# Earlier loads and an earlier dispatch in the last block of an attention and soft-MoE kernel

## The chip, the cores and the metric

One core of one Trainium2 chip runs the whole program. The metric is the device time of one execution in microseconds (us). A time given as "at 525.7" counts from the first instruction of the profiled execution.

## What is computed

Three layers follow each other, all in 32-bit floats.

```python
# q, k, v: (8, 8, 576, 64), attention inside chunks of 64 tokens
scores = q_c @ k_c.T / sqrt(64);  out = softmax(scores) @ v_c
x = out.transpose(0, 2, 1, 3).reshape(4608, 512)
# first MLP
h = x @ w_in                              # 512 -> 2048
x = (h / (1 + exp(-1.702 * h))) @ w_out   # 2048 -> 512
# soft mixture of experts, 8 experts of 4 slots
logits = x @ phi                          # (4608, 32)
d = softmax(logits, axis=0)               # dispatch weights, over all tokens
slot_in = d.T @ x                         # (32, 512)
slot_out[e] = relu(slot_in[e] @ w1[e]) @ w2[e]   # w1: 512x1024, w2: 1024x512
out = softmax(logits, axis=1) @ slot_out  # combine weights, over the slots
```

## The kernel before

The 4608 tokens are cut into 12 blocks of 384 (block 0 to block 11). A block has 16 columns, one for each 128 features of the first MLP. `block(b)` runs the columns in order: `gemm(b, f)` does the 12 matmuls of column f, the tanh on ScalarE and the gelu product on VectorE; then `side(b, f)` adds what a hand-written plan puts at that column, and `at` issues the weight loads that `TABLE` names for it. The order of calls is the order of instructions on every engine. Nothing is reordered later; an instruction starts when its data and its buffer are there and its engine's queue has come to it.

`w_out` is not applied to the tokens. The dispatch works on the gelu values: `dispatch(b)` multiplies the block's dispatch weights with the gelu values turned by 90 degrees and adds the result to `acc`, and `w_out` comes once at the end. The turned gelu goes a long way in blocks 1 to 10: `store_g` turns 32x32 squares on VectorE into a buffer for 4 columns (`g1`), and stores it to DRAM in four transfers of 192 KB; in the block after, `load_g` loads the four quarters (`g2`, 768 KB each) back. In the last block there is no block after, so `gemm_t` turns the gelu on TensorE, two columns late, and VectorE copies it out.

For block b the steps of the softmax over tokens and slots are run in block b+1: `S0` (`slots_0`: the logits by one matmul, their maximum, a transposed copy), `S1` (`slots_1`: two exponentials on ScalarE), `S2` (`slots_2`: the dispatch weights `dt`, turned by four VectorE instructions), `S3` and `S4` (`slots_3`, `slots_b`: the combine weights, normalized, turned and stored to `ct_dram` in small pieces of 128 bytes by three transfers). `d0` is the dispatch and `g0` the load of the gelu. `PLAN` holds the columns for the ordinary blocks, `LAST` those of block 11. So block 11 does the work of block 10's softmax and dispatch, its own logits (`l0` to `l2`) and its own gemm.

The experts' weights (33.5 MB) are loaded from block 9 on into whatever buffer comes free. `TABLE` gives the order of buffer kinds: `w` is a buffer of `w_in` that a column of block 11 has used up, `s` a slab, `m` a small buffer, and so on. The loads of blocks 10 and 11 are issued by GpSimd, one behind the other, each waiting for its buffer. Gelu stores, gelu loads and combine-weight stores are issued by SyncE in the order of the program.

There are 11 slabs (`NSLAB`). The two halves of a block's tokens (`xh`, `xl`), `g1`, `g2`, the turned gelu of the last block (`g2t`, one slab for 4 columns), the `s` loads and the output tiles share them.

The `tail()` turns block 11's last columns, does its softmax and dispatch, applies `w_out`, runs the experts (`up`, `turn`, `down`) and combines. The twelve output tiles of 768 KB are stored by GpSimd (the first nine) and SyncE (the last three).

Of the kernel before, what the change touches and what calls it, by code (L numbers as in the profile page):

```python
# [17 lines left out]
T = 384  # L18
# [5 lines left out]
NW = 17  # L24
ROOM = {'w': 4, 's': 6, 'q': 4, 'v': 2, 'x': 2, 'p': 6, 'm': 2, 't': 2, 'k': 2, 'c': 4}
TABLE = {
    '9.15': 'cwxx', '10.6': 'q', '10.11': 'vq', '10.12': 't', '10.14': 'sst', '10.15': 'v', '11.0': 'w', '11.3': 's', '11.10': 'ss',
    'a': 'ssmk', 'b': 'ssss', 'e': 'ppppp',
}
TABLE.update({f'11.{f}': TABLE.get(f'11.{f}', '') + 'w' for f in range(1, 16)})  # L30
TABLE.update({f'11.{f}': TABLE[f'11.{f}'] + 'm' for f in range(10, 16)})
TABLE['11.15'] += 'm'
TABLE['11.5'] = ''.join(TABLE.pop(f'11.{f}') for f in (2, 3, 4, 5))
EVAC = 'vvvvvvvvvvvvvvav'
LAST = (('g0', 2), ('l3', 4), ('l0', 4), ('S0', 5), ('S1', 6), ('S2', 7), ('S3', 8), ('S4', 8), ('d0', 9), ('l1', 8), ('l2', 12))

# [50 lines left out]
def attention_moe_softmoe_kernel(  # L89
# [16 lines left out]
    NF = DFF // 128  # L106
    NB = NT // T
    NCP = T // 128
    GF = 4
    NG = NF // GF  # L110
# [19 lines left out]
    def slab_tile(shape, dtype, name):  # L130
        return slab.tile(shape, dtype, tag="s", name=name)
# [186 lines left out]
    def attn_e(cp, pool):  # L318
        exp(cp)
        for _ in steps_f(cp, pool):  # L320
            pass
# [35 lines left out]
    def attn_b(cp):  # L357
        if cp >= TURN:
            t = pt[cp] = ptp.tile([128, 2 * KD, 64], F32, tag="p", name="pt_sb")
            nc.vector.transpose(out=t.rearrange("p a k -> p (a k)"), in_=et.pop(cp).rearrange("p a k -> p (a k)"))  # L360
        else:
            attn_t(cp)
            attn_p(cp)
# [69 lines left out]
    gt, g1, g2, g2t, gh = {}, {}, {}, {}, {}  # L433
# [45 lines left out]

    g_dram = {}  # L480

    def load_g(b):
        g2[b] = []
        for q in range(NG):
            t = slab_tile([128, 4, NCP, GF * 32], F32, f"g2_{q}")
            nc.sync.dma_start(
                out=t.rearrange("p q a c -> p (q a c)"), in_=g_dram.pop((b, q)).rearrange("b p q x -> (b p) (q x)")
            )
            g2[b].append([t[:, :, i, :] for i in range(NCP)])
# [20 lines left out]
    def logits(b, g):  # L510
        if g == 0:
            lp[b] = ps.tile([128, T], F32, tag="lp" if b % 2 or b == 0 else "pt", name="lp")
        for j in range(4):
            f = 4 * g + j
            nc.tensor.matmul(  # L515
                out=lp[b][32 * j:32 * (j + 1), :], lhsT=wp[:, f, :], rhs=gt[b, f],
                start=(g == 0), stop=(g == NG - 1),
            )
        if g == NG - 1:
            p = lp.pop(b)  # L520
            if b == NB - 1:
                lps[b] = [mid_tile([128, T], "lps")]
                nc.scalar.activation(out=lps[b][0], in_=p, func=ACTF.Copy)
                return
            lps[b] = [
                mid_tile([128, T], f"lps{i}", F32R) if b else pro[0].tile([128, T], F32R, tag="gt", name="lps0", bufs=NF)
                for i in range(2)
            ]
            nc.scalar.activation(out=lps[b][0], in_=p, func=ACTF.Copy)
            nc.vector.tensor_tensor(out=lps[b][1], in0=p, in1=lps[b][0].bitcast(F32), op=ALU.subtract)  # L530
# [101 lines left out]
    def slots_n(b):  # L632
        lt = lg_t[b]
        cs = st_p.tile([128, NCP, 1], F32, tag="cs", name="cs")
        nc.vector.tensor_reduce(out=cs, in_=lt, axis=AX.X, op=ALU.add)
        nc.vector.tensor_scalar_add(out=cs, in0=cs, scalar1=EPS)
        nc.vector.reciprocal(out=cs, in_=cs)
        nc.vector.tensor_tensor(out=lt, in0=lt, in1=cs.to_broadcast([128, NCP, 32]), op=ALU.mult)

    def slots_b(b):  # L640
        slots_n(b)
        lt = lg_t[b] if b == NB - 2 else lg_t.pop(b)
        t = st_p.tile([128, NCP, 32], F32, tag="ct", name="ct_b")
        nc.vector.transpose(out=t, in_=lt)
        for a in range(NCP):
            k, r = divmod(b * NCP + a, 4)
            if k == NT // 512 - 1:
                continue
            nc.sync.dma_start(out=ct_dram[r, :, k].rearrange("s j c -> j s c"), in_=t[:, a, :])

    def dispatch(b):
        dt, cr = dt_t.pop(b)
        g = g2.pop(b)
        p = ps.tile([128, 512], F32, tag="m", name="dtg")
        for i in range(NCP):
            for j in reversed(range(4)):
                nc.tensor.matmul(  # L657
                    out=p[32 * j:32 * (j + 1)], lhsT=dt[:, i, :], rhs=g[j][i], start=(i == 0), stop=(i == NCP - 1)
                )
        if b == FIRST:  # L660
            nc.vector.tensor_copy(acc, p)
        else:
            nc.vector.scalar_tensor_tensor(out=acc, in0=acc, scalar=cr, in1=p, op0=ALU.mult, op1=ALU.add)
# [94 lines left out]
    def more_wo():  # L758
        if wo_list:
            fn, i = wo_list.pop(0)  # L760
            fn(i)
# [227 lines left out]
    def side(b, f):  # L989
        for name, at in (LAST if b == NB - 1 else PLAN):  # L990
            if b == 2:
                at = {"g0": 9, "d0": 15, "b1": 5}.get(name, at)
            if b == 3:
                at = {"b3": 14}.get(name, at)
            if f != at:
                continue
            kind, i = name[0], int(name[1:])
            if kind == "l":
                if i == NG - 1:
                    logits(b - 1, i)  # L1000
                else:
                    logits(b, i)
            elif kind == "S":
                (slots_0, slots_1, slots_2, slots_3, slots_b)[i](b - 1)
            elif kind == "d":
                dispatch(b - 1)
            elif kind == "g":
                load_g(b - 1)
            elif kind == "w":
                if NPRO <= b < 10:  # L1010
                    more_wo()
            elif kind == "p":
                cp = (b + 1) * NCP + i
                pair_step(cp if cp < NB * NCP else None, cp - 2)
            elif (b + 1) * NCP + i < NB * NCP:
                cp = (b + 1) * NCP + i
                if kind == "e":
                    attn_e(cp, True)
                else:
                    attn_b(cp)  # L1020
# [15 lines left out]
    def pair_step(a, c, early=False):  # L1036
        t = pair_tile("sx")
        if a is not None:
            y = attn_s(a, t[:, :, 0:256])
        if c is not None:  # L1040
            z = attn_x(c, t[:, :, 256:512])
        if early and c is not None:
            attn_y(c, z)
        if a is not None:
            attn_m(a, y)
            if a > 5:
                load_qk(a + 2)
        if c is not None:
            if not early:
                attn_y(c, z)  # L1050
            if c > 5:
                load_v(c + 2)
# [67 lines left out]
    def start(steps):  # L1120
        fns = {
            "i": w_in_a, "h": w_in_h, "I": w_in_b, "j": w_in_c, "u": w_in_d, "o": wp_a, "q": load_qk, "v": load_v, "b": attn_b, "c": wp_c, "d": wp_d,
            "W": spin, "t": lambda f: store_g(0, f), "k": lambda g: logits(0, g), "l": lambda g: logits(1, g),
            "S": lambda i: (slots_0, slots_1, slots_2, slots_3, slots_b)[i](0),
        }
        once = {
            "phi": start_wp, "z": start_const, "s": start_sel, "G": lambda: load_g(0), "D": lambda: dispatch(0),
        }
        for x in steps.split():
            k, n = x[0], x[1:].rstrip("rp")  # L1130
            if x in once:
                once[x]()
            elif k == "L":
                load_w(x[1], int(n[1:]), x[-1])
            elif k == "P":
                pair_step(*[None if y == "-" else int(y) for y in n.split(",")], early=True)
            elif k == "e":
                attn_e(int(n), x[-1] != "r")
            else:
                fns[k](int(n))  # L1140
# [15 lines left out]
    def block(b):  # L1156
        for f in range(NF):
            gemm(b, f)
            if b == NB - 1 and f > 1:
                gemm_t(b, f - 2)  # L1160
            side(b, f)
            if b < 5:
                start((SIDE2, SIDE3, SIDE4)[b - 2].get(f, ""))
            at(f"{b}.{f}")
# [87 lines left out]
```

## Time and profile before

| | us |
|---|---|
| median of 3 runs | 626.5 (624.05 to 626.56) |
| the profiled execution's own time | 625.01 |
| its span, first to last instruction | 623.2 |
| TensorE busy | 606.0 |
| VectorE busy | 471.6 |
| ScalarE busy | 217.3 |
| GpSimd busy | 182.5 |

The span is what the trace covers; about 1.8 us of the execution's own time lie outside it. TensorE (PE) is busy in 97% of the span. Its granted clock is 0.995 of full speed over the span.

### The profile page before, as it was taken

The page shows a single profiled execution, that of the slowest core. Times are in us where ns is not written, and L with a number is a line of the kernel's source. Part 1 is how long each engine was busy: PE and PEld are TensorE (multiplying, and loading weights), DVE is VectorE, ACT ScalarE, POOL GpSimd, SP SyncE. Part 2 cuts the span into 40 slices and gives each one's busy share as a digit, 9 for nine tenths or more (in the row PEclk, how much of TensorE's full clock was granted, in tenths as well). Part 3 has the DMA queues.
Part 4 walks back from the last instruction along what each step waited for, and adds up shares of the span by engine and source line. Part 5 has one row for each costly group of instructions (what it writes and reads, how often), then busy time and mean ns, then how long its engine had stood idle before and what let it go on. Part 6 is the DMA issues. An engine that isn't in the chain of part 4 may idle for free.

```text
span 623.2 us, 15697 instructions
## 1 busy us (share of the span) xinstructions
PE 606.0 (97%) x6430; PEld 515.4 (83%) x6430; DVE 471.6 (76%) x1007; ACT 217.3 (35%) x461; POOL 182.5 (29%) x299
## 2 busy tenths in 40 slices
PE   8999999999999999999999999999999999989993
PEld 7899888888898798898979889989989798766652
DVE  6999698789788888998888889888877746343152
ACT  4986345232232332322333332423322322121152
POOL 1010010334134134154143333342441331353320
PEclk9999999999999999999999999999999999999998
DMA  8983785559799686795695794876839889899998
GB/s 343 398 313 122 232 306 152 134 134 363 189 358 290 230 279 217 199 339 179 183 348 169 238 325 146 289 241 166 329 96 305 288 259 414 293 356 411 409 390 336
DMA packets 64535, 167.81 MB, mean 269 GB/s; under 512 B 11536, under 2 KB 34064, under 8 KB 64464
## 3 DMA queue, kind: packets, MB, share of 16 engines
q1 hardware_dynamic: 54864, 127.75, 61.9%
q0 software_dynamic: 9600, 39.06, 16.3%
q8 instruction: 50, 0.82, 0.5%
q14 instruction: 21, 0.17, 0.1%
HBM read 122.22 MB, written 44.56 MB: 268 GB/s over the span
## 4 chain that ended last, share of the span: by engine, by line
PE 89%; DMA 7%; DVE 1%; SPq 1%; ACT 0%; issue 0%; DVEq 0%; ACTq 0%
PE h L445 62%; PE lp L515 5%; PE dtg L657 5%; DMA g<-g_dram 5%; PE sx L294 3%; PE fp L897 2%; PE h1p L859 2%; PE sx L387 2%; PE op L972 2%; DMA stg<-in_moe_w_in_dram 2%; DMA qv<-in_qk_dram 1%; PE wpp L238 1%; PE sx L400 1%; PE sip L812 1%; PE pt L372 1%; PE lg L538 1%
## 5 line engine op out<-in xcount | busy, mean ns | idle before, releaser
L445 PE MATMUL h<-xh,w 128*128 128x384 f32 x1536 | 396.2, 339 | 1.2 <-ACT xh L424 1.2
L445 PEld LDWEIGHTS h<-xh,w 128*128 128x128 f32 x1536 | 273.7, 188 | 26.6 <-issue 22.7
L445 PE MATMUL h<-xl,w 128*128 128x384 f32 x768 | 256.8, 335 | 0.0
L352 POOL TENSOR_TENSOR es<-e,rs 32x256 f32<-32x256 f32 x208 | 131.0, 630 | 242.9 <-DVE rs L335 193.1
L454 ACT ACTIVATE gt<-h 128x384 f32<-128x384 f32 x192 | 93.7, 489 | 221.9 <-PE h L445 221.7
L458 DVE SCALAR_TENSOR_TENSOR gt<-gt,h 128x384 f32<-128x384 f32 x192 | 103.4, 539 | 56.6 <-ACT gt L454 55.6
L445 PEld LDWEIGHTS h<-xl,w 128*128 128x128 f32 x768 | 144.1, 188 | 0.1
L467 DVE STREAM_TRANSPOSE g<-gt 128x384 f32<-128x384 f32 x176 | 100.5, 575 | 7.4 <-PE dtg L657 1.8
L424 ACT ACTIVATE xh<-sx 128x512 fp32r<-128x512 f32 (+1 forms) x38 | 21.5, 574 | 74.9 <-DVE e L313 44.3
L341 POOL TENSOR_TENSOR e<-e,rs 128x512 f32<-128x512 f32 x9 | 10.3, 1146 | 100.8 <-DVE rs L335 88.9
L515 PE MATMUL lp<-gt,wp 128*32 128x384 f32 x384 | 39.0, 493 | 0.0
L429 DVE TENSOR_TENSOR xl<-sx,xh 128x512 fp32r<-128x512 f32 (+1 forms) x38 | 24.8, 657 | 18.3 <-ACT xh L424 17.6
L657 PE MATMUL dtg<-g,dt 128*32 128x512 f32 x264 | 31.0, 596 | 1.7 <-DMA g<-g_dram 1.7
L737 POOL DMA_DIRECT2D w<-in_moe_w_dram x33 | 17.7, 538 | 45.7 <-PE h L445 26.9
L310 DVE TENSOR_REDUCE mx<-sx 128x8 f32<-128x512 f32 (+1 forms) x38 | 23.8, 631 | 7.0 <-PE sx L294 7.0
L313 DVE TENSOR_TENSOR e<-sx,mx 128x512 f32<-128x512 f32 (+1 forms) x38 | 25.0, 662 | 1.2
L325 ACT ACTIVATE e<-e 128x512 f32<-128x512 f32 x36 | 22.6, 628 | 7.6 <-DVE e L313 7.4
L743 POOL DMA_DIRECT2D w<-in_moe_w_dram x33 | 17.6, 535 | 22.0 <-DMA w<-in_moe_w_dram 13.3
L330 DVE TENSOR_REDUCE sm<-e 128x8 f32<-128x512 f32 x36 | 23.4, 650 | 0.0
L294 PEld LDWEIGHTS sx<-qk 64*64 64x64 f32 x960 | 16.7, 134 | 7.7 <-issue 7.4
L515 PEld LDWEIGHTS lp<-gt,wp 128*32 128x32 f32 x384 | 10.7, 109 | 13.1 <-issue 8.6
L657 PEld LDWEIGHTS dtg<-g,dt 128*32 128x32 f32 x264 | 8.2, 109 | 15.9 <-issue 13.8
(132 smaller groups left out, 546.1 us busy)
## 6 DMA issues: line engine op xcount, KB each, us to landing
g_dram<-g SPq DMA_DIRECT2D x176, 192.0 KB, 3.4
g<-g_dram SPq DMA_DIRECT2D x44, 768.0 KB, 8.7
w<-in_moe_w_dram POOLq DMA_DIRECT2D x37, 512.0 KB, 7.4
qk<-in_qk_dram SPq DMA_DIRECT2D x30, 512.0 KB, 10.3
stg<-in_moe_w_in_dram SPq DMA_DIRECT2D x16, 512.0 KB, 6.1
stg<-in_moe_w_out_t_dram SPq DMA_DIRECT2D x16, 512.0 KB, 5.6
wo<-in_moe_w_out_dram SPq DMA_DIRECT2D x16, 512.0 KB, 3.7
v<-in_v_dram SPq DMA_DIRECT2D x30, 256.0 KB, 8.5
```

The lines of the kernel that those rows point to most:

```text
L294: nc.tensor.matmul(out=y[h][w, hp, :], lhsT=t[r, 0, hp, w], rhs=t[r, 1, hp, w], start=True, stop=True)
L310: nc.vector.tensor_reduce(out=mx[:, hs], in_=v, axis=AX.X, op=ALU.max)
L313: nc.vector.tensor_tensor(out=ev[:, hs], in0=v, in1=mx[:, hs].to_broadcast(list(v.shape)), op=ALU.subtract)
L330: nc.vector.tensor_reduce(out=sm, in_=e, axis=AX.X, op=ALU.add)
L352: nc.gpsimd.tensor_tensor(out=t[w, :, 32 * i:32 * i + 32], in0=e[r, :, 32 * j:32 * j + 32], in1=rs[r].to_broadcast([32, 2 * KD, 32]), op=A ...
L429: nc.vector.tensor_tensor(out=l, in0=v, in1=h.bitcast(F32), op=ALU.subtract)
L445: nc.tensor.matmul(out=h, lhsT=w_t[f][:, (0, 1, 0)[p], k, :], rhs=(xh, xh, xl)[p][b][:, k, :], start=(i == 0), stop=(i + 1 == len(steps)),)
L454: nc.scalar.activation(out=gt[b, f], in_=gh[b, f], func=ACTF.Tanh, scale=0.851)
L458: nc.vector.scalar_tensor_tensor(out=t, in0=t, scalar=1.0, in1=gh.pop((b, f)), op0=ALU.add, op1=ALU.mult)
L467: nc.vector.transpose(out=g1[b, q][:, :, :, 32 * j:32 * (j + 1)], in_=t.rearrange("p (a b c) -> p b a c", b=4, c=32))
L515: nc.tensor.matmul(out=lp[b][32 * j:32 * (j + 1), :], lhsT=wp[:, f, :], rhs=gt[b, f], start=(g == 0), stop=(g == NG - 1),)
L657: nc.tensor.matmul(out=p[32 * j:32 * (j + 1)], lhsT=dt[:, i, :], rhs=g[j][i], start=(i == 0), stop=(i == NCP - 1))
```

## The change

Four things are changed in the last block and around it.

1. The load of block 10's gelu is split. Quarters 0, 1 and 2 (`G0`, `G1`, `G2`) are issued at column 0 of block 11, quarter 3 (`G3`) at column 2. Before, all four were issued at column 2.
2. `S4` of block 9, which normalizes and stores its combine weights, goes from column 15 of block 10 to column 0 of block 11, behind `G0` to `G2` (`T0`).
3. The dispatch of block 10 (`d0`) goes from column 9 to column 7, `S1` from 6 to 5, `S2` from 7 to 6.
4. In the table of weight loads one slab of the first two at the tail's start (`a`) and the two slabs of column 10 are replaced by three slabs at column 7, and at each column the `w` load comes ahead of the `s` loads.

```diff
-    '9.15': 'cwxx', '10.6': 'q', '10.11': 'vq', '10.12': 't', '10.14': 'sst', '10.15': 'v', '11.0': 'w', '11.3': 's', '11.10': 'ss',
-    'a': 'ssmk', 'b': 'ssss', 'e': 'ppppp',
+    '9.15': 'cwxx', '10.6': 'q', '10.11': 'vq', '10.12': 't', '10.14': 'sst', '10.15': 'v', '11.0': 'w', '11.3': 's', '11.7': 'sss',
+    'a': 'smk', 'b': 'ssss', 'e': 'ppppp',
 }
-TABLE.update({f'11.{f}': TABLE.get(f'11.{f}', '') + 'w' for f in range(1, 16)})
+TABLE.update({f'11.{f}': 'w' + TABLE.get(f'11.{f}', '') for f in range(1, 16)})
...
-LAST = (('g0', 2), ('l3', 4), ('l0', 4), ('S0', 5), ('S1', 6), ('S2', 7), ('S3', 8), ('S4', 8), ('d0', 9), ('l1', 8), ('l2', 12))
+LAST = (('G0', 0), ('G1', 0), ('G2', 0), ('T0', 0), ('G3', 2), ('l3', 4), ('l0', 4), ('S0', 5), ('S1', 5), ('S2', 6), ('d0', 7), ('S3', 8), ('S4', 8), ('l1', 8), ('l2', 12))
...
-    def load_g(b):
-        g2[b] = []
-        for q in range(NG):
+    def load_g(b, qs=range(NG)):
+        g2.setdefault(b, [])
+        for q in qs:
...
+            if b == NB - 2:
+                at = {"S4": NF}.get(name, at)
...
+            elif kind == "T":
+                slots_b(b - 2)
             elif kind == "g":
                 load_g(b - 1)
+            elif kind == "G":
+                load_g(b - 1, (i,))
```

## Rows read from the trace of the kernel before

**Rows 1.** The page: engines' busy time, and DMA busy in tenths of 40 slices.
```profile
PE 606.0 (97%) x6430; PEld 515.4 (83%) x6430; DVE 471.6 (76%) x1007; ACT 217.3 (35%) x461; POOL 182.5 (29%) x299
...
DMA  8983785559799686795695794876839889899998
```
**Rows 2.** Busy time by stretch: us, engines' busy (instructions), clock, DMA share, GB/s.
```profile
515.00:528.00 13.00, 13.00 (x88) 11.56 (x86) 7.59 (x20) 3.45 (x9) 2.11 (x4) 1.00 1.02 416
528.00:532.70 4.70, 3.54 (x25) 2.57 (x23) 3.54 (x12) 1.12 (x3) 1.05 (x2) 1.00 0.99 396
532.70:538.00 5.30, 5.24 (x40) 3.31 (x40) 0.84 (x2) 0.12 (x1) 1.87 (x4) 1.00 0.54 165
...
556.00:596.00 40.00, 39.50 (x666) 24.93 (x666) 10.42 (x31) 6.60 (x19) 12.67 (x24) 1.00 1.01 401
```
**Rows 3.** The chain that ended last, 500 to 560: start, us, what.
```profile
514.04 18.58 DMA g<-g_dram
```
**Rows 4.** Timeline of TensorE: start, us, instruction, idle before and releaser.
```profile
525.22 0.49 PE L500 MATMUL gtp<-ident,gt 128*128 128x128 f32 x3
...
531.05 0.49 PE L500 MATMUL gtp<-ident,gt 128*128 128x128 f32 x3
532.76 2.78 PE L657 MATMUL dtg<-g,dt 128*32 128x512 f32 x24 [1.22 <-DMA g<-g_dram]
```
**Rows 5.** Timeline of SyncE's issues around the end of block 10.
```profile
506.80 2.18 SPq L474 DMA_DIRECT2D g_dram<-g  x4
509.08 2.41 SPq L649 DMA_DIRECT2D ct_dram<-ct_b  x3
...
511.59 2.77 SPq L486 DMA_DIRECT2D g<-g_dram  x4
```
**Rows 6.** What SyncE's queue waited for, 505 to 536: us, times, longest.
```profile
SPq L486 <- DMA g_dram<-g: 0.4, 1, 0.4
```
**Rows 7.** DMA traffic from 511.55 to 515: packets by size, and SyncE's queue.
```profile
DMA packets 790, 1.29 MB, mean 375 GB/s; under 512 B 365, under 2 KB 555, under 8 KB 790
...
q1 hardware_dynamic: 524, 0.33, 30.0%
```
**Rows 8.** The same from 515 to 528: SyncE's (q1) and GpSimd's (q0) queue.
```profile
q1 hardware_dynamic: 647, 3.06, 57.1%
q0 software_dynamic: 648, 2.33, 44.6%
```
**Rows 9.** The same from 528 to 532.7: SyncE's queue.
```profile
q1 hardware_dynamic: 23, 0.10, 5.1%
```
**Rows 10.** Issue to landing (median us): loads issued at 511.59, 521 to 528, 535.84, 599.56.
```profile
g<-g_dram SPq DMA_DIRECT2D x1, 768.0 KB, 12.0
...
w<-in_moe_w_dram POOLq DMA_DIRECT2D x3, 512.0 KB, 8.9
...
w<-in_moe_w_dram POOLq DMA_DIRECT2D x1, 512.0 KB, 3.7
...
out_dram<-o POOLq DMA_DIRECT2D x1, 768.0 KB, 5.1
```
**Rows 11.** Timeline of VectorE: combine weights of block 9, and steps of block 11.
```profile
507.65 0.28 DVE L644 STREAM_TRANSPOSE ct_b<-lt 128x96 f32<-128x96 f32 x1
...
522.34 1.15 DVE L546 STREAM_TRANSPOSE lt<-lg 32x96 f32<-32x96 f32 x4
...
526.88 1.11 DVE L566 STREAM_TRANSPOSE dt<-d 32x96 f32<-32x96 f32 x4
```
**Rows 12.** Timeline of GpSimd's issues in block 11.
```profile
525.68 0.53 POOL L737 DMA_DIRECT2D w<-in_moe_w_dram  x1 [1.89 <-PE h L445]
...
535.84 0.53 POOL L737 DMA_DIRECT2D w<-in_moe_w_dram  x1 [3.53 <-PE dtg L657]
```
**Rows 13.** Timeline of all engines at the end of block 11's last column.
```profile
550.78 0.82 PE L500 MATMUL gtp<-ident,gt 128*128 128x128 f32 x6
...
551.50 0.56 DVE L458 SCALAR_TENSOR_TENSOR gt<-gt,h 128x384 f32<-128x384 f32 x1 [1.40 <-ACT gt L454]
```

## What the change was predicted to do

> **What bounds the kernel now.** I read the page first: TensorE is busy 606.0 of 623.2 us, and the DMA engines are nearly full over the last sixth of the span [rows 1]. So there are two things to look for near the end: the few holes in TensorE's work, and the places where the DMA queue sets the time. The table by stretch has both. In block 11 TensorE is full from 515 to 528, has a hole between 528 and 532.7, and from 556 to 596 it is busy 39.50 of 40 us although the DMA share is 1.01 there [rows 2]. The weights thus arrive in time in the tail, and nothing is gained by bringing them earlier as such. The hole is the wait of block 10's dispatch for its gelu: 1.22 us, released by the load [rows 4]. The chain that ended last goes through that load, 18.58 us from its issue at 514.04, so it landed at 532.62 [rows 3]. That is the fourth quarter; the first one, issued at 511.59, took 12.0 us [rows 10]. I chose this load as the centre of the argument, since everything the change moves meets there.
>
> The very end is DMA-bound. Twelve output tiles of 768 KB leave back to back. The third, issued at 599.56, took 5.1 us; a 512 KB load into a quiet queue took 3.7 us [rows 10]. With 256 KB more at 401 GB/s [rows 2] (0.65 us) the third tile could have landed 0.7 us earlier, had nothing stood before it. So if TensorE is later by D, the end is later by D less about 0.7 (an estimate); if TensorE is earlier, the end follows as far as the weights in front of the outputs do.
>
> **The dispatch, two columns earlier.** Columns end with the transposes: the dispatch of column 9 was ready at 531.05 + 0.49 = 531.54, that of column 7 will be at 525.22 + 0.49 = 525.71 [rows 4], as the work before it is the same. That is 5.83 us earlier. To stall no longer than the old 1.22 us, the last quarter must land by 526.9, or 5.7 us earlier than it did.
>
> **What brings the loads forward.** SyncE issues in order: block 10's last four stores from 506.80 to 508.98, three combine-weight stores (T0's) to 511.49, then four loads from 511.59 [rows 5]. With the change G0 to G2 come right behind the stores, at about 509.1: 2.5 us earlier. G3 isn't earlier. It needs the last store landed; before, SyncE waited 0.4 us for just that [rows 6] and issued it at 514.04, and this stays. Between G2 and G3 now stand T0's three stores: 2.41 us of SyncE's time, from about 510.9 to 513.3, so beside G3's wait.
>
> When do the bytes move? From 511.55 to 515 SyncE's queue moved 0.33 MB in 524 packets, mostly small ones: the stores' rest and T0's [rows 7]. So the loads' data began at 515, 3.4 us after the first issue. From 515 to 528 that queue moved 3.06 of the 3.15 MB, 235 GB/s, with GpSimd's weights taking the other half [rows 8] and the engines full, share 1.02 [rows 2]. With G0 issued at 509.1 the data could begin at 512.5, but the stores ahead of it in the same queue move until about 513 (the last had landed by 514.04). So the loads begin 2.0 to 2.5 us earlier and run at the same pace, since both queues are full either way; I take 2.2. The bulk is through at 525.8 instead of 528.0.
>
> The last 0.10 MB, 23 packets, took until 532.6 [rows 9]: a lag of 4.6 us, with some of the DMA engines behind the rest. T0's small packets, which stood ahead of all loads, are the likely cause. They now stand between G2 and G3, and where they partly ran in the gap before 515, they now run against a full weight queue. Bounds for the landing of G3: 526.3, if the small packets cost nothing; 530.4, if the lag is the same (532.6 less 2.2); 534.6 above, when the last weight load issued before the dispatch (column 7, 525.68 [rows 12]) has landed at that time's median of 8.9 us [rows 10] and nothing is left to compete. I take 531.5, a quarter of the way from the same lag to the upper bound.
>
> The Trainium skill ("DMA: Bandwidth & Descriptors", section "Why a DMA increments its semaphore by 16 and not by 1") says that a SyncE transfer runs on as many of the 16 engines as divide its outermost dimension. By it each of T0's stores, whose outermost size is 4, sits on four engines, which would make a few engines late. The 23 late packets agree; no row here names an engine.
>
> Stall at 531.5: 531.5 - 525.7 = 5.8 us, against 1.22. **TensorE is later by 4.6.**
>
> **Dispatch weights.** `dt` took four turns of VectorE at 526.88 to 527.99 in column 7 [rows 11]. In column 6 they come about two microseconds earlier, near 526.0 (the two exponentials of S1 now also sit before column 6's tanh). Alone that stalls the dispatch by 0.3 us; behind G3 it costs nothing.
>
> **T0's VectorE work**, five instructions ending at 507.93 [rows 11], goes behind column 0's gelu. Nobody on TensorE waits for it: nothing.
>
> **The slabs.** Before, loads waited for the dispatch until 535.84 [rows 12]; after, three slabs are issued when the dispatch ends (531.5 + 2.78 = 534.3), with the later `w` loads queued behind them. This fills part of the DMA hole from 532.7 to 538, where the share was 0.54 [rows 2], with 768 KB more than before; but the tail did not wait for weights, so it is worth nothing while TensorE is late. It has a price. Counting slabs: two of tokens, two and one of weights, four of gelu, two of turned gelu are all eleven. The dispatch frees four; three go to weights, one to the third `g2t`. The fourth `g2t` (column 14) then waits for the tokens, that is for the last gemm. VectorE's copy goes behind it, beside column 15's tanh, and the next transposes (x6 at 550.78) and the gelu at 551.50 [rows 13] queue behind the copy. From nothing (hidden by tanh) to 0.6 us (copy not hidden at all); I take 0.2.
>
> **Sum:** 4.6 + 0.2 - 0.7 = +4.1 us. The profiled execution's 625.0 becomes 629.1. The median of the runs is 1.5 above that execution, so as a median 626.5 + 4.1 = 630.6. A change below 0.5%, 3.1 us, can't well be told from none here.
>
> **Rivals.** (A) The forecast: G3 lands between 529.5 and 534.6, a stall of 3.8 to 8.9, so +2.1 to +7.2: 628.6 to 633.7. For it: G3's issue does not move, and the dispatch moves 5.83 us where the data move 2.2. Against it: the lag's cause is not shown.
>
> (B) The lag shrinks, because the small packets no longer hold up the first three quarters. G3 lands at 526.3 to 528.5, the stall is 0.6 to 2.8: TensorE -0.6 to +1.6, the end between -0.6 and +1.1: 625.9 to 627.6. It decides from a landing below 530.5, where the loss falls under 3.1 us.
>
> (C) All quarters are in place by 525.7. Only `dt`'s 0.3 is left, so TensorE gains 0.9; with the DMA hole filled (0.46 of 5.3 us, 2.4 us) the end may follow by up to 1.5: 625.0 to 625.6. For faster by 0.5% even this is too little: 1.22 us is all that the hole holds, and the outputs' queue gives the rest. Against it: 235 GB/s for 3.15 MB is 13.4 us, and there are 12.7 to 13.2 us from the start of the data.
>
> The same page of the Trainium skill (section "Anatomy of one DMA", on transfers that GpSimd issues) fits a load as about 2.0 us plus its bytes at 436 GB/s, which would be 3.8 us for a quarter, an estimate: G3 would be there at 518 and (C) would hold. The trace is against it here: 12.0 and 18.58 us.
>
> (D) The small packets crawl behind weights for longer than the upper bound, over 8.9 us of stall: 634 and more.
>
> **Chances.** A 0.56, B 0.26, C 0.12, D 0.06. Slower by over 0.5% holds for most of A (G3 after 530.5, 0.44) and D: 0.50. Within 0.5%: the rest of A, B and most of C: 0.45. Faster: 0.05. The range leaves out D, the top of A and the lower part of C: 625.4 to 632.8; A's own is 628.6 to 633.7.
>
> **What will show it.** In the profile after: the dispatch (L657, 24 matmuls) near 531 instead of 532.76 with an idle time of 4 to 6 us before it, released by a load of the gelu; the loads' issues on SyncE at 509 and one at 514; G3's landing. Then the tail's steps later by the extra stall and the same length. I am wrong if the dispatch starts before 528, if its wait is named as `dt`, or if the tail itself grows by a wait for weights or for the fourth `g2t`.

## The result and the profile after

The changed kernel takes 631.6 us (median of 4 runs, 631.13 to 631.83) where the kernel before took 625.3 beside it (623.32 to 626.56): a ratio of 1.0103, 95% interval 1.0069 to 1.0136. It is slower by 6.3 us and lies inside the range of the forecast (628.6 to 633.7). The forecast of 630.6 was 4.1 us added to a median of 626.5; part of its closeness to 631.6 comes from the kernel before, whose median was 1.2 lower this time. The profiled execution took 631.55 us, 6.54 more than the profiled one before; its span is 629.8 us.

The page after: busy time of the engines, then TensorE and its granted clock in 40 slices of the span.

```profile
PE 607.7 (96%) x6430; PEld 515.9 (82%) x6430; DVE 472.5 (75%) x1007; ACT 217.0 (34%) x461; POOL 182.5 (29%) x299
...
PE   8999999999999999999999999999999995989993
...
PEclk9999999999999999999999999999999997999998
```
TensorE's work grew by only 1.7 us, yet one slice late in the span fell to 5 tenths busy, and the clock fell in the same slice. So the time went into one hole, and something happened to the clock there. The timeline of TensorE after, to set beside [rows 4]:

```profile
525.16 0.49 PE L500 MATMUL gtp<-ident,gt 128*128 128x128 f32 x3
531.95 4.51 PE L657 MATMUL dtg<-g,dt 128*32 128x512 f32 x24 [6.31 <-DMA g<-g_dram]
```
The dispatch is ready at 525.65 and waits 6.31 us for the load, against 1.22 before. The same 24 matmuls then take 4.51 us in place of 2.78. The table by stretch after, with the columns of [rows 2]:

```profile
515.00:525.60 10.60, 10.60 (x73) 9.10 (x71) 5.37 (x14) 2.95 (x8) 2.56 (x5) 1.00 1.02 414
525.70:531.90 6.20, 0.00 (x0) 0.00 (x0) 2.60 (x10) 0.15 (x1) 0.44 (x1) 0.74 0.93 369
531.90:537.00 5.10, 5.05 (x27) 1.72 (x28) 0.39 (x1) 0.00 (x0) 0.26 (x1) 0.65 0.01 5
537.00:543.00 6.00, 6.00 (x41) 5.14 (x40) 2.69 (x9) 1.15 (x3) 3.98 (x8) 1.00 0.79 257
...
528.70:535.40 6.70, 3.45 (x20) 0.96 (x24) 0.00 (x0) 0.00 (x0) 0.00 (x0) 0.50 0.40 163
```
In the stretch in which TensorE did nothing the granted clock fell. It is 0.50, the lower of the chip's two levels (1.2 GHz is half of 2.4 GHz), from 528.7 to 535.4, and then 1.00 again; over the 5.1 us from the start of the dispatch this makes a mean of 0.65. All of [rows 2] were at 1.00. The chain of waits after goes through the load as in [rows 3], but with another issue time:

```profile
517.65 14.17 DMA g<-g_dram
531.95 4.51 PE dtg L657 x24
...
562.89 2.13 PE dtg L782 x33
```
G3 landed at 531.82. Its issue, however, is at 517.65 and not at 514. SyncE's issues after show why, beside [rows 5]:

```profile
494.97 13.95 SPq L474 DMA_DIRECT2D g_dram<-g  x8
509.01 1.91 SPq L486 DMA_DIRECT2D g<-g_dram  x3
510.98 6.56 SPq L649 DMA_DIRECT2D ct_dram<-ct_b  x3
517.65 5.14 SPq L486 DMA_DIRECT2D g<-g_dram  x1
```
T0's three stores took 6.56 us of SyncE's time (2.41 before), of which 5.44 went into the third, and G3's own issue then took 5.14. Last, the DMA traffic of each queue after, as [rows 8] and [rows 9] give it, for 521.8 to 526 and then for 526 to 531.9:

```profile
q0 software_dynamic: 467, 1.66, 98.8%
q1 hardware_dynamic: 120, 0.02, 2.6%
...
q0 software_dynamic: 379, 1.36, 57.2%
q1 hardware_dynamic: 411, 0.82, 35.8%
```
For 4.2 us SyncE's queue (q1) moved nothing but 120 small packets of 0.02 MB, while GpSimd's weights had 98.8% of the engines. G3's 0.79 MB came almost all behind 526.

The balance up to the tail: its first dispatch group (L782) starts at 562.89 where it started at 556.12, 6.77 later. The stall is 5.09 longer and the dispatch 1.73: 6.82, of which 0.06 goes off because column 7 ended that much earlier (525.16 for 525.22).

### The profile page after: what moved, and what is told of

Same layout as the page of the kernel before. It is cut to its first block, busy times and chain, and to the rows that moved or that the text cites. A ratio compares the mean times of both kernels' runs of the same rounds, so it can differ in the third digit from the quotient of the medians.

```text
span 629.8 us, 15702 instructions
## 1 busy us (share of the span) xinstructions
PE 607.7 (96%) x6430; PEld 515.9 (82%) x6430; DVE 472.5 (75%) x1007; ACT 217.0 (34%) x461; POOL 182.5 (29%) x299
## 4 chain that ended last, share of the span: by engine, by line
PE 88%; DMA 7%; DVE 3%; ACT 1%; issue 0%; SPq 0%; DVEq 0%; ACTq 0%
PE h L445 60%; PE lp L515 5%; PE dtg L657 5%; DMA g<-g_dram 4%; PE sx L294 3%; PE fp L897 2%; PE h1p L859 2%; PE op L972 2%; PE sx L387 2%; DMA stg<-in_moe_w_in_dram 2%; DMA qv<-in_qk_dram 1%; PE wpp L238 1%; PE sx L400 1%; PE gtp L500 1%; PE sip L812 1%; PE pt L372 1%
## 5 line engine op out<-in xcount | busy, mean ns | idle before, releaser
L657 PE MATMUL dtg<-g,dt 128*32 128x512 f32 x264 | 32.8, 625 | 6.8 <-DMA g<-g_dram 6.6
```

What stands on the lines that cost most here:

```text
L657: nc.tensor.matmul(out=p[32 * j:32 * (j + 1)], lhsT=dt[:, i, :], rhs=g[j][i], start=(i == 0), stop=(i == NCP - 1))
```

## The experiments

Three groups were run, each beside its own runs of the kernel before (medians 623.7, 624.2 and 623.4 us). All ratios are against those. "Own stall" is the idle time in front of the dispatch in the run's profile.

| run | median us | ratio, 95% interval | own stall | dispatch took |
|---|---|---|---|---|
| dispatch back at column 9 | 623.96 | 1.0004 (0.9993 to 1.0015) | 0.49 | 2.78 |
| T0 behind loads and dispatch | 624.61 | 1.0015 (1.0004 to 1.0025) | 1.40, for dt, then the load | 2.78 |
| TensorE kept busy, 40 matmuls | 631.43 | 1.0116 (1.0096 to 1.0137) | 2.01 | 2.78 |
| weights held back | 626.12 | 1.0029 (1.0009 to 1.0048) | 1.23, for dt | 2.78 |
| before, T0 at column 10 | 623.51 | 0.9993 (0.9984 to 1.0002) | none | 2.78 |
| before, dispatch at column 7 | 629.57 | 1.0095 (1.0079 to 1.0112) | 3.70 | 4.48 |
| dispatch at 8, T0 at 10 | 623.17 | 0.9984 (0.9971 to 0.9997) | none | 2.78 |
| TensorE kept busy, 58 matmuls | 630.03 | 1.0103 (1.0087 to 1.0119) | none | 2.78 |
| T0's stores issued by GpSimd | 624.78 | 1.0012 (0.9998 to 1.0026) | 1.23, for dt | 2.78 |
| changed kernel, old table | 632.32 | 1.0129 (1.0103 to 1.0154) | 6.55 | 4.58 |

One of the ten runs with GpSimd's issues took 1343 us and is left out of its interval; what held it is not known. Times of different runs can be set side by side only to within some tenths: the transposes that end column 7 start at 525.22 before and at 525.16 after, and between 524.47 (T0's stores issued by GpSimd) and 525.44 (dispatch at column 7) in the other profiles, as the work ahead of the last block varies.

**Dispatch back at column 9**, in the changed kernel, its three slabs with it.
```diff
-('S2', 6), ('d0', 7), ('S3', 8), ('S4', 8),
+('S2', 6), ('S3', 8), ('S4', 8), ('d0', 9),
-'11.7': 'sss'
+'11.9': 'sss'
```


> The changed kernel with the dispatch back at column 9 and its three slabs of weights with it; loads, T0 and S0 to S2 as changed. Queue theory (T0's small packets stand between G2 and G3 and hold G3 up): G3 still lands near 531.8, the dispatch is ready at 531.5, stall 0.3 us, dispatch 2.8 us at full clock; 624.5 to 625.5 us, 6 to 7 below the changed kernel. Distance theory (the loads need that long anyway, the dispatch is just too early): the same, this run doesn't tell the two apart. Slab theory (the three slabs and the order of weight loads cost the time): still over 628.

The whole loss is gone: 1.0004. SyncE's issues are those of the changed kernel, but the dispatch is ready when the load is almost there:
```profile
511.31 6.44 SPq L649 DMA_DIRECT2D ct_dram<-ct_b  x3
517.86 5.16 SPq L486 DMA_DIRECT2D g<-g_dram  x1
```
```profile
532.17 2.78 PE L657 MATMUL dtg<-g,dt 128*32 128x512 f32 x24 [0.49 <-DMA g<-g_dram]
```
So the changed load order, with G3 landed at 532.03, is with the dispatch at column 9 neither better nor worse than the old one. What costs is asking for the data two columns earlier.

**T0 behind loads and dispatch**, in the changed kernel.
```diff
-('G2', 0), ('T0', 0), ('G3', 2), ..., ('d0', 7), ('S3', 8),
+('G2', 0), ('G3', 2), ..., ('d0', 7), ('T0', 8), ('S3', 8),
```


> The changed kernel with T0 at column 8, behind all four loads and the dispatch, instead of between G2 and G3. Queue theory: G3 is issued near 513.8 and lands by 525.5 to 526.5; the dispatch at column 7 waits 0.3 to 1 us and takes 2.8 us; 624 to 625.5 us. Distance theory: with the weights taking half of the engines G3 lands at 528 to 531 all the same, stall 3 to 6 us; 628 to 631.

Beside the kernel before it loses 0.9 us, so 5.5 of the 6.3 come back. G3 is issued at 514.05, as the prediction had it, and lands 13.1 us later, at 527.1:
```profile
509.24 5.13 SPq L486 DMA_DIRECT2D g<-g_dram  x4
```
```profile
527.27 2.78 PE L657 MATMUL dtg<-g,dt 128*32 128x512 f32 x24 [1.40 <-DVE sum L568]
```
```profile
525.89 1.11 DVE L566 STREAM_TRANSPOSE dt<-d 32x96 f32<-32x96 f32 x4
```
With T0 gone from between the loads, 4.7 us of the landing are gone too. The landing is still a little later than the 525.5 to 526.5 that was expected, and the wait longer. The wait has two ends close together. It is named after VectorE's sum, which the dispatch does not read; `dt` was turned at 527.00, G3 landed at 527.1, and the dispatch started at 527.27. In two runs below it starts 0.10 us after `dt`, so here the load ended the wait, by about 0.2 us. Why the whole kernel is 0.9 us slower than before with a stall only 0.2 us longer isn't shown.

**TensorE kept busy in the stall**, in the changed kernel: matmuls into an unused buffer stand ahead of the dispatch. It was run twice, with 40 matmuls and, as these covered only 4.5 us of the stall, with 58.
```diff
             elif kind == "d":
+                if b == NB - 1:
+                    spin(40)
                 dispatch(b - 1)
```


> The changed kernel with 40 idle transposes on TensorE ahead of the dispatch, so that it works through most of the stall. Clock theory (the dispatch took 4.51 instead of 2.78 us because the granted clock had fallen in the stall): G3 lands at 531.8 as before, the dispatch takes 2.8 us, 629.9 us, 1.7 below the changed kernel. Rival (the dispatch was slow because the landing data or the weights' traffic slowed its reads): still 4.5 us and 631.6.

> The changed kernel with 58 idle transposes (6.5 us at the rate of the 40) ahead of the dispatch, which fill the whole stall. Clock theory: no run loses the clock, the dispatch takes 2.8 us; 629.5 to 630.2 in all runs, against 629.99 to 632.04 with 40 transposes, where 2 us stayed idle. If runs still reach 631.5, the clock's fall has another cause.

With 40, three of four runs were no faster than the changed kernel and one was, at 629.99 us. That is the profiled one: with 2.01 us of idle time left, its dispatch took 2.78 us. Its mean granted clock was 0.995, and 0.991 to 0.993 in the other three; the changed kernel's four runs had 0.990 or 0.991. With 58, all four runs lie between 629.96 and 630.43, at 0.994 to 0.996. Timeline and table by stretch of TensorE with 58:
```profile
525.20 6.50 PE L1066 MATMUL spin<-ident 128*128 128x128 f32 x58
531.75 2.78 PE L657 MATMUL dtg<-g,dt 128*32 128x512 f32 x24
```
```profile
525.70:531.70 6.00, 5.99 (x55) 5.75 (x53) 2.34 (x8) 0.00 (x0) 0.16 (x1) 1.00 0.91 361
531.70:537.00 5.30, 5.25 (x39) 3.09 (x39) 0.75 (x1) 0.15 (x1) 1.85 (x4) 1.00 0.18 49
```
The load lands as late as ever and nothing useful is done in the stall, yet the dispatch is 1.73 us shorter and the tail starts at 560.93 in place of 562.89 (0.3 of this is the earlier start of the columns). The rival of the expectation, that landing data or the weights slow the dispatch's reads, is out: both are here as before. The runs lie 1.6 us below the changed kernel's (630.0 for 631.6). The two ratios, both 1.0103, don't tell them apart, as the kernel before had a higher median beside the changed kernel (625.3 from 4 runs, 624.2 from 20 here); so the price of the clock rests on the profiles, on these times and on the clocks of the single runs.

**Weights held back**, in the changed kernel: the six `w` loads of columns 2 to 7 and the slab of column 3, 3.9 MB, go behind the dispatch (the expectation's 3.4 MB is too low).
```diff
-TABLE['11.5'] = ''.join(TABLE.pop(f'11.{f}') for f in (2, 3, 4, 5))
+TABLE['11.7'] = 'ssss' + 'w' * 6
+for f in (2, 3, 4, 5, 6):
+    TABLE.pop(f'11.{f}')
```


> The changed kernel with the weight loads of columns 2 to 6 (3.4 MB) held back behind the dispatch, so that SyncE's queue has the DMA engines almost for itself. Queue theory: the small packets lose their competitor, T0's three stores pass within 2 to 3 us, SyncE is not held up, G3 lands by 521, stall at most 0.5 us. Distance theory: G3 is also earlier, by 525. If G3 still lands after 529, small packets are slow by themselves and not by sharing. The total is open, since 3.4 MB of weights move into the tail: 624 to 632.

The load is in place in time, though at 524.7 and not by 521, and the wait for `dt` alone is what is left of the stall. The weights held back are missed later: the tail starts at 555.91, where it started before if the 0.2 us of earlier columns are taken off, but the median is 2.4 us longer, and in the tail TensorE waits 1.7 us for weights, which it does neither before nor in the changed kernel. Against the expectation SyncE was still held in T0's stores, though the next issue took 2.27 us and not 5.14:
```profile
511.08 5.73 SPq L651 DMA_DIRECT2D ct_dram<-ct_b  x3
516.93 2.27 SPq L488 DMA_DIRECT2D g<-g_dram  x1
```
```profile
526.70 2.78 PE L659 MATMUL dtg<-g,dt 128*32 128x512 f32 x24 [1.23 <-issue]
```
The weights issued before column 2 still moved then, so this run doesn't tell whether the hold needs them. What the later weights decide is how T0's small packets fare: its three stores landed between 521.9 and 522.9 here, and between 526.3 and 529.1 in the changed kernel.

**T0 alone, and the dispatch alone**, in the kernel before.
```diff
 T0 alone (with the lines that take S4 out of block 10 and know "T")
-('d0', 9), ('l1', 8), ('l2', 12))
+('d0', 9), ('l1', 8), ('l2', 12), ('T0', 10))
 dispatch alone
-('S1', 6), ('S2', 7), ('S3', 8), ('S4', 8), ('d0', 9),
+('S1', 5), ('S2', 6), ('d0', 7), ('S3', 8), ('S4', 8),
```


> The kernel before with one edit: T0 (block 9's combine weights) goes from column 15 of block 10 to column 10 of block 11, behind the loads and the dispatch, which stays at column 9. Queue theory: the four loads are issued from 509 on with no small packets ahead, G3 at 514, and land by 527 instead of 532.6; the dispatch at 531.5 does not wait; 1.2 us are gained on TensorE, 0.5 to 1.2 at the end. Distance theory (the loads need until 531 in any case): G3 lands at 530 to 531, gain the same or less. If the end does not move although TensorE gains 1.2 us, the outputs' DMA sets it.

> The kernel before with the dispatch at column 7, S1 at 5 and S2 at 6, and nothing else: the loads stand behind T0 as before and the table of weights is the old one. If moving the dispatch is the whole loss: G3 lands at 532.6 as before, stall 6.9 us, the clock falls, the dispatch takes 4.5 us; 7 us over before. If T0's place between G2 and G3 is what costs: clearly less than the changed kernel's 6.3 to 7.9, since T0 stands ahead of the loads here.

T0 alone takes the old stall away. G3 is issued at 513.70 and lands in 13.0 us, 5.9 earlier than before:
```profile
508.83 5.19 SPq L486 DMA_DIRECT2D g<-g_dram  x4
```
```profile
531.22 2.78 PE L657 MATMUL dtg<-g,dt 128*32 128x512 f32 x24
```
The tail starts 1.55 us earlier (554.57; 0.25 of it is the earlier start of the columns), but the median shows only 0.7 us of it, with an interval that still includes 1. The dispatch alone costs 5.3 us. Chain and table by stretch of that run:
```profile
514.14 15.35 DMA g<-g_dram
...
529.63 4.48 PE dtg L657 x24
```
```profile
529.60:534.50 4.90, 4.87 (x27) 1.71 (x28) 0.33 (x1) 0.00 (x0) 0.00 (x0) 0.65 0.45 179
```
Behind 3.70 us of idle time the clock was down here too. The same issues as in [rows 5] landed G3 in 15.35 us here and in 18.58 there, so the lag behind T0 is no constant. This puts the 5.3 us between the two expectations, and the run does not share out the loss. Set together: with the dispatch at column 7 the loss is 5.3 us with T0 ahead of all four loads, 6.3 with T0 between G2 and G3 and 0.9 with T0 behind them; with the dispatch at column 9 no place of T0 loses.

**T0's stores issued by GpSimd**, in the changed kernel; nothing is left out or moved in the order of the program, but the stores now stand ahead of GpSimd's weight loads.
```diff
-    def slots_b(b):
+    def slots_b(b, eng=nc.sync):
-            nc.sync.dma_start(out=ct_dram[...], in_=t[:, a, :])
+            eng.dma_start(out=ct_dram[...], in_=t[:, a, :])
-                slots_b(b - 2)
+                slots_b(b - 2, nc.gpsimd)
```


> The changed kernel with T0's three small stores issued by GpSimd at the same column, so that SyncE's queue holds only G0 to G3. Issue theory (G3 is late because SyncE sat in T0's third store until 517.5 and in G3's own issue until 522.8): G3 is issued near 514 and lands by 527 on all engines, the dispatch waits 1.2 us for dt or the load and takes 2.8 us; 624 to 625.5 us. Sharing theory (the small packets slow the engines whoever issues them): G3 still lands after 529 and the stall is over 3.5 us.

SyncE is free again. The four loads are issued in 3.12 us, G3 at 511.08, 6.6 earlier than in the changed kernel (0.7 of it is the earlier start of the columns), and it lands in 12.5 us, at 523.6:
```profile
508.28 3.12 SPq L486 DMA_DIRECT2D g<-g_dram  x4
```
```profile
526.19 2.78 PE L657 MATMUL dtg<-g,dt 128*32 128x512 f32 x24 [1.23 <-issue]
```
```profile
524.98 1.11 DVE L566 STREAM_TRANSPOSE dt<-d 32x96 f32<-32x96 f32 x4
```
The dispatch starts 0.10 us after the last turn of `dt`. Everything else of the change is in place, and all but 1.4 us of the loss is gone, with an interval that includes 1. But G3's issue is 3 us ahead of the 514 that was expected, and that is not SyncE's doing. GpSimd waits in front of T0's stores, and three weight loads, issued at 507.36, 509.44 and 511.52 in the changed kernel, leave only from 511.08:
```profile
508.97 2.12 POOL L649 DMA_DIRECT2D ct_dram<-ct_b  x3 [8.31 <-DVE ct_b L644]
511.08 1.67 POOL L737 DMA_DIRECT2D w<-in_moe_w_dram  x3
```
Beside fewer weights the last gelu store, for which G3 waits, left its last landing mark at 510.99 and not at 513.77. So this run moves weights as well as T0, and alone it doesn't prove that SyncE's hold was the cause; the run with T0 at column 8, where G3 is issued at 514.05 and lands at 527.1, has no such shift. The two together say that at column 7 the load can be had in time, and the wait for `dt` that remains, 1.23 us, is just what the kernel before waited.

**The old table**, in the changed kernel.
```diff
-'11.7': 'sss', ... 'a': 'smk'        f'11.{f}': 'w' + ...
+'11.10': 'ss', ... 'a': 'ssmk'       f'11.{f}': ... + 'w'
```


> The changed kernel with the old table of weight loads (two slabs at column 10, two at the tail's start, s ahead of w). Queue theory: the slabs are worth nothing either way; dispatch at 532, 4.5 us long; 631.0 to 632.2 us. Slab theory: with the old table the time falls to 629 or below.

No better than the new one: stall 6.55, dispatch 4.58. The slabs are not where the time went. The median is 0.1 us over the range that was expected, and the profiled execution took 633.02. In it the tail's own dispatch was slow too:
```profile
562.69 4.46 PE L782 MATMUL dtg<-g,dt 128*32 128x256 f32 x48 [1.38 <-DVE dt L610]
```
In the eleven other profiles it took 2.80 us at a clock of 1.00, behind the same wait of 1.38 us; here the clock was 0.63 from 562.6 to 567.2. This is 1.66 us of the 633.02, and no row ties it to the slabs.

**Dispatch at column 8, T0 at column 10**, in the changed kernel, the version that the others point to.
```diff
-('T0', 0), ..., ('d0', 7), ('S3', 8), ('S4', 8), ('l1', 8), ('l2', 12))
+('d0', 8), ('S3', 8), ('S4', 8), ('l1', 8), ('T0', 10), ('l2', 12))
-'11.7': 'sss'
+'11.8': 'sss'
```


> The changed kernel with the dispatch and its three slabs at column 8, and T0 at column 10. Loads land by 527.1 as in the run with T0 at column 8, dt is ready at 527, the dispatch of column 8 is ready at 528.1: no wait, full clock; TensorE ends 1.2 us ahead of before; 0.5 to 1.5 us under before. If the outputs' DMA sets the end, no more than 0.5.

No stall, the tail starts at 554.67, and it is the one run that is clear of noise on the fast side: 1.1 us below the kernel before.
```profile
527.82 0.49 PE L500 MATMUL gtp<-ident,gt 128*128 128x128 f32 x3
528.24 1.06 PE L657 MATMUL dtg<-g,dt 128*32 128x512 f32 x8
```

## Why the prediction came out, step by step

**Right: what decides.** Rival A held. The dispatch was ready 5.89 us earlier (525.65 for 531.54), its last quarter came 0.8 earlier, and G3 landed at 531.82 where 531.5 was written. The stall of 6.31 lay a little over the 4 to 6 us that were named as the sign. That column 9 gives the loss back and that the dispatch alone costs 5.3 us shows it.

**Right: the start of the data.** The loads' bytes began near 512.6 and not at 515, 2.4 us earlier where 2.2 were taken. G0 to G2 had landed by 522.8.

**Wrong: "G3 isn't earlier ... and this stays".** The step gave T0's stores 2.41 us "beside G3's wait", so G3 would be issued at 514.04. It was issued at 517.65, since T0's third store held SyncE for 5.44 us. With T0 behind the loads the issue is at 514.05, which is the 514.04 of the prediction without T0's hold. That the landing came out at 531.8 all the same is luck, two errors that offset: the lag was drawn from [rows 9] and its cause put down to small packets in front of the bulk, while here a late issue and small packets in front of G3 itself took the same time, in shares that no run separates. What SyncE waits for in these issues isn't shown; that its queue may hold only so much is an inference that no run tests.

**Right in kind: the small packets.** They did crawl against the weights, from 521.8 to 529. Each of T0's stores left one mark in the trace right behind its issue and four as its data landed, where G3 left sixteen: eleven by 529.8, one at 530.6, and the last four from 531.5 to 531.8. This is what the Trainium skill ("DMA: Bandwidth & Descriptors", section "Why a DMA increments its semaphore by 16 and not by 1") makes of an outermost size of 4, and here the trace agrees with it: the load ends with four engines that were late. It leaves one thing open: G3's issue was over at 522.79, and until 526 SyncE's queue moved small packets alone. These can hold four engines; why the twelve others had no bytes of G3 yet isn't shown.

**Missing: the clock.** The sum had a stall and no more. A stall of 6.31 us also made the dispatch behind it 1.73 us longer, which the run with 58 matmuls gives back.

**Mis-sized: `dt`.** 0.3 was written, worked out from `dt` near 526.0. Its four turns started at 525.66 and took 1.11, after ScalarE's exponentials had waited 2.8 us for VectorE:
```profile
ACT d L554 <- DVE lt L546: 2.8, 1, 2.8
```
```profile
525.66 1.11 DVE L566 STREAM_TRANSPOSE dt<-d 32x96 f32<-32x96 f32 x4
```
Alone it is 1.23 us. Rival C's gain of 0.9 was therefore not to be had at column 7 at all: the best case there is the old wait.

**Mis-sized: two small terms.** The fourth `g2t` cost nothing. VectorE's copy did wait for the last gemm, but the gelu follows the transposes by 0.72 us, as in [rows 13], and 5.34 us lie between the transposes and the tail's dispatch (L782) in both kernels:
```profile
557.55 1.19 PE L500 MATMUL gtp<-ident,gt 128*128 128x128 f32 x6
557.58 0.56 DVE L504 COPY g<-gtp 128x384 f32<-128x384 f32 x1 [1.16 <-PE h L445]
...
558.27 0.56 DVE L458 SCALAR_TENSOR_TENSOR gt<-gt,h 128x384 f32<-128x384 f32 x1
```
The outputs' slack gave 0.2 (6.77 at the tail, 6.54 at the end), not 0.7.

From forecast to measurement: 4.1, plus 0.5 of stall (5.09 for 4.6), plus 1.7 for the clock, less 0.2 for `g2t`, plus 0.5 of slack that wasn't there, is 6.6.

## What to carry to other kernels

Before moving a consumer forward, put its new time beside the landing of its last input and beside every other input in turn: here the load was 6 us late, and behind it `dt` was late by all that could have been won. A short store between two loads of one queue is not priced by its bytes; small packets behind loads and beside a full weight queue delayed the next load's issue and its landing, so such a store belongs after the data that someone waits for. Price a stall of TensorE of some microseconds with the slower clock of the work that follows it.

## What the runs showed of the hardware beside that

- **Turns by packet.** From 521.8 to 526, 467 packets of GpSimd's queue on 16 engines are 29 for each, or 25 without the 62 of them that are under 512 bytes, and 120 small packets of SyncE's on four engines are 30 for each. So a packet of 128 bytes seems to have cost its queue a turn against one of 4 KB. The Trainium skill (the same page, section "Queues, rings and completion order") says that an engine goes round its queues packet by packet; these counts agree with it in kind. A packet of the Trainium skill there is a group of descriptors, and no row shows whether the packets counted here are such groups.
- **An issue can block.** SyncE's issue of one transfer took 5.1 to 5.5 us with transfers of its queue under way, in each of the five profiles with T0 between G2 and G3 and the full weights, where T0's first two stores took some 0.5 us each. In the run with T0 at column 8 one of five stores took 4.25 us; in the two runs with T0 at column 10 none took over 0.58.
- **Idle time and the clock.** Stalls of 1.2 to 1.4 us left block 10's dispatch at 2.78 us; behind 3.70 us it took 4.48 and behind 6.31 us 4.51. At 2.01 us it was 2.78 in the one run that has a profile, while the other three runs of that kernel were 1.2 to 2.0 us longer at a lower mean clock. A short wait is no safe one either: behind the tail's 1.38 us the clock stayed up in eleven profiles and was down in the one with the old table. Five runs of the kernel before had a mean clock of 0.991 or 0.992 and took 624.4 to 627.6 us, where most had 0.994 to 0.996; where it fell in them isn't to be seen without a profile.
